# Polysketch attention and a tanh-shrink FFN on one core: the first 256 tokens head by head, a new order of the work, and 1.45 MB of loads in flight

## The chip, the core and the metric

One core of a Trainium2 chip. The metric is the device time of one execution in microseconds. Five engines take part: PE (TensorE, matmuls), DVE (VectorE), ACT (ScalarE), POOL (GpSimd) and SP (SyncE, which issues nearly all DMAs). Each works through its own queue of instructions strictly in order, and waits on semaphores where an operand comes from another engine or from a load.

## What is computed

```python
# q, k, v: 4 batches, 4 heads, 1088 tokens, 32 features; S1, S2: 8 x 32
def phi(x):                     # 64 features: products of two sketches of 8
    a = einsum('rd,bhsd->bhsr', S1, x)
    b = einsum('rd,bhsd->bhsr', S2, x)
    return einsum('bhsi,bhsj->bhsij', a, b).reshape(..., 64)
q_p, k_p = phi(q), phi(k)
kv  = einsum('bhsf,bhsd->bhfd', k_p, v)
z   = sum(k_p, axis=2)
num = einsum('bhsf,bhfd->bhsd', q_p, kv)
den = einsum('bhsf,bhf->bhs', q_p, z) + 1e-6
x   = (num / den), heads side by side       # 4352 tokens x 128
h   = x @ w_in                              # 128 x 2048
out = (h - tanh(h)) @ w_out                 # 2048 x 128, float32
```

Every key of a batch enters its kv, so that no token of a batch can be finished before all its keys and values are there.

## The kernel before

All matmuls of the attention are float32 in small tiles of the array (32x32, 64x32, 128x32); those of the FFN are bf16 on the whole array. The kernel first records all operations with their operands, and then a table (`TABLE`) lists them one by one in a global order; each token names the operation, the engine that gets it (v DVE, a ACT, g POOL, t PE, s SP) and, after the colon, the buffers. `f` and `F` are filler matmuls on zeros. From the table every engine gets its queue, and the waits follow from the operands and the buffers.

Loads stand in SP's queue in the table's order. `plan` also makes a load wait until the loads issued before it have landed but for the newest ones, so that no more than `CAP` bytes are in flight:

```python
if o.big:
    left = CAP - o.dma[0]
    for p in reversed(loads):
        left -= p.dma[0]
        if left < 0:
            o.deps.setdefault(p, False)
            break
    loads.append(o)
```

For each batch (b = 0 to 3) the attention runs through these steps; the names are those that the text uses, with batch and place (kT2, qp1.5), and the lines are those of the profile:

- keys: load kL (L438), turn on DVE (kT, L528), sketch on PE (ksk, L548), turn on DVE (abk, two instructions, L554; called kab in the order);
- gram matrix on PE (gram, L569), copy (gm, L579), the denominators' weights on PE (scmm, L575), copy into the query weights (L581);
- products of the two key sketches (w, three pieces of 128x768, L589, on DVE or POOL), kv on PE (kvmm, three pieces, L604, into one bank, 128x64);
- kv into the form that the numerator needs: copied four times side by side (kvd), transposed by PE (kvt, L622), copied (kvb);
- queries: load qL, turn on DVE (qT, L540), sketch on PE (qsk, L643), turn on DVE (abc, L648); products and sums for the denominator (m L660, den L663), reciprocal (rd, L666), scaled half (ap, L668; called aq in the order); products (qp, L686), turned (qpT, L691);
- numerator on PE (num, L702, which writes four banks), and two copies into xT in bf16 (L349).

Numerators come in pieces of whole blocks of 128 tokens: batch 0 has (0, 2), (2, 5) and (5, 9); batch 1 (0, 5) and (5, 9); batches 2 and 3 one. Batch 0's first 256 tokens have a query load, sketch and products of their own.

The weights: wi and wo are loaded as float32 in four pieces each and cast to bf16; wi is transposed by PE (wit, L767; copies wiT), and `w_in @ w_out` is made from both (wc, L781) and split into two bf16 parts (wch, wcl L788), because `h - tanh(h)` times w_out is computed as `x @ (w_in @ w_out)` plus `tanh(-h) @ w_out`. wc lies in one of the three banks that the hidden layer uses, until wcl has read it.

The FFN runs over ten groups of tokens (256, 384, 448, six of 512, 192), numbered 0 to 9. A group has 16 hidden matmuls (h, L802), 16 tanh on ACT (th, L806; from group 7 on two at a time), and 18 output matmuls (o, L817 and L821) that collect in one bank, which DVE turns (ot, L826) and SP stores in four DMAs (st, L836). Group 0 needs the tokens 0 to 256, group 1 those to 640, group 2 those to 1088 (all of batch 0), group 3 those to 1600. In the table of before, the kv work of batches 1, 2 and 3 (kT, ksk, abk, w, kvmm, kvt) stands between group 0's end and group 2's beginning.

Of the kernel before, what the change touches and what calls it, by code (L numbers as in the profile page):

```python
# [4 lines left out]
B, H, S, D = 4, 4, 1088, 32  # L5
# [18 lines left out]
TABLE = """
0v 50g 14s 13a 10g 1g 15s 6g 2g 16s 17s 18s 19s 20s 59v:0 21s 4v 22s 60v 23s 61v 48v 5v 51g 62v 8g 52g 7g 49v f F F F
F F F F F F F 64t:0 58g 24s 3g 25s 65v:0 63v 66v F F F F F F 67t:0 71v:0 68a:0 f F 69t 72v:1 74t:1 70a 80t:0 75t 73v:2
26s 225a 81v:0 F F 233t:0 27s 226a 82g:0 11g 28s 83v:0 234t 227a 84v:0 29s 85g:0 76t 86g:0 236t:1 30s 77a:0 31s 78t
229a 53g 12g 87v:0 228g 79a:0 32s F F 88t:0 235a 55g 91v 237t 89a 90a 230g 33s 100t:0 238a 245t:0 231g 34s 247t:2
101v:1 246a:0 249t:1 248a:1 251t:0 232g 35s 250a:2 253t:2 277t:0 252a:3 36s 255t:1 278t 102v:0 254a:4 257t:0 37s
256a:5 259t:2 103v:1 279t 258a:6 261t:1 38s 260a:7 104v:1 263t:0 262a:8 39s 105g:1 265t:2 264a:9 239t:1 280t 266a:10  # L30
54g 267t:0 56g 106v:1 240t 40s 269t:2 268a:11 281t 282t 270a:12 271t:0 111g:2 283t 284t 107v:1 241t 272a:13 41s 285t
273t:2 286t 287t 42s 275t:0 274a:14 113g:0 108t:0 112v:0 276a:15 43s 242t 114v 109a 44s 110a 115t:0 118v:1 45s 119v
46s 300t:0 302t:2 116a 288t 47s 157v:0 120t:0 301a:16 243a 303a:17 289t 244v 92s 304t:0 290t 121v:1 291t 306t:1
305a:18 292t 122v 293t 307a:19 117v 127g:3 158v 294t 308t:0 310t:1 295v:0 159t:0 128g:4 309a:0 296s 311a:1 312t:0 93s
332t:0 160v:0 333t 94s 313a:2 334t 314t:1 136v 129g:5 316t:2 95s 318t:0 315a:3 335t 130t:0 297s 317a:4 96s 123t:2 161v
319a:5 131t 97s 124a:1 162t:1 166g:0 298s 191v:1 132t 299s 125t 336t 98s 192v 320t:0 126a 133a:1 337t 99s 322t:1 9g
168v:1 321a:6 134t 193t:1 323a:7 167g:2 163a:0 135a:1 324t:0 338t 194v:1 339t 325a:8 326t:1 328t:2 195v 169t:0 327a:9
200v:3 196t:2 329a:10 170t 164t 171t 201v:4 165a 340t 330t:0 341t 342t 202v:5 331a:11 203t:1 197a:1 204t 172v:0 198t
205t 175v 199a 173t 206a:1 343t 344t 207t 174a:2 355t:0 209v 357t:1 208a:3 345t 137t:0 356a:12 358a:13 359t:0 361t:1
138v:0 346t 360a:14 347t 363t:2 348t 362a:15 349t 365t:0 364a:16 367t:1 176t:0 350v:1 139g:0 366a:17 351s 368a:18  # L40
387t:0 140v:0 369t:0 352s 388t 389t 141v:0 353s 370a:19 371t:1 390t 142v:0 354s 373t:2 372a:0 391t 177v:1 143g:1 392t
374a:1 375t:0 393t 377t:1 376a:2 394t 395t 378a:3 379t:2 396t 145g:2 144v:1 397t 380a:4 398t 399t 381t:0 383t:1 57g
400t 150g:0 146v 382a:5 385t:2 401t 384a:6 147t:0 386a:7 152g:1 151v:0 402t 403t 149v 148a 404t 153v 410t:0 412t:1
414t:2 178v:1 411a:8 154t:0 413a:9 179v:1 415a:10 180v:1 416t:0 181g:1 155v 418t:1 156a 420t:2 417a:11 405v:2 210t:0
182g:2 419a:12 406s 422t:0 421a:13 442t:0 407s 211v:0 424t:1 423a:14 426t:2 408s 443t 425a:15 444t 409s 428t:0 445t
427a:16 184v:0 446t 430t:1 429a:17 447t 432t:2 212g:0 183v:1 431a:18 448t 434t:0 433a:19 449t 436t:1 213v:0 450t
435a:0 438t:2 214v:0 451t 437a:1 452t 186v:1 440t:0 439a:2 453t 465t:1 441a:3 454t 185v 455t 467t:2 466a:4 456t 457t
187v 468a:5 469t:0 458t 459t 470a:6 471t:1 215v:0 473t:2 460v:0 218g:2 475t:0 472a:7 188t:0 474a:8 461s 476a:9 462s
220g:0 463s 477t:0 497t:0 479t:1 464s 478a:10 498t 499t 480a:11 481t:0 216v:1 483t:2 500t 482a:12 485t:1 501t 484a:13
217v:0 502t 487t:0 486a:14 503t 489t:2 189v 504t 488a:15 505t 491t:1 490a:16 190v 493t:0 506t 492a:17 507t 219v 508t  # L50
495t:2 494a:18 520t:1 509t 496a:19 221v 510t 522t:0 521a:0 524t:2 511t 523a:1 512t 526t:1 513t 525a:2 514t 528t:0
527a:3 530t:2 515v:1 222t:0 529a:4 516s 531a:5 517s 532t:0 518s 552t:0 534t:1 533a:6 519s 536t:2 553t 535a:7 554t 555t
537a:8 538t:0 540t:1 556t 539a:9 542t:2 557t 541a:10 544t:0 558t 543a:11 559t 546t:1 560t 545a:12 548t:2 561t 547a:13
550t:0 562t 549a:14 563t 564t 579t:1 551a:15 565t 581t:2 580a:16 566t 583t:0 582a:17 585t:1 567t 584a:18 568t 569t
# [855 lines left out]
```

## Time and profile before

| | |
|---|---|
| time, three runs | 111.40, 112.95 and 112.78 us; median 112.78 |
| profiled execution | 111.28 us, span of the trace 109.1 us |
| PE busy | 97.9 us (90%) |
| ACT busy | 80.8 us (74%) |
| DVE busy | 58.4 us (54%) |
| POOL busy | 30.3 us (28%) |
| moved by DMA | 11.38 MB, mean 104 GB/s |

In the profile's rows the columns are the start in us, the duration, the engine, the line and the operation, what is written from what, the shapes, and how many instructions the row merges; in brackets stands the idle time of the engine ahead of it and what ended that. SPq is SP's queue issuing a DMA. A float32 matmul of the small tiles is shown as two. Matmuls overlap: a row of one 512-column matmul lasts 0.38 us, but the next starts 0.22 us after it. A busy PE is therefore not one at its peak.

### The profile page before, as it was taken

To read this page: it belongs to the slowest core of one execution; us is meant where nothing else is said; L and a number is where in the kernel's file an instruction comes from. 1 tells how busy PE (TensorE), PEld (TensorE's weight loads), DVE (VectorE), ACT (ScalarE), POOL (GpSimd) and SP (SyncE) were. 2 spreads that over 40 slices of the span, in tenths; PEclk is the share of its full clock that TensorE was granted. 3 is DMA by queue.
4 is the path that set the end of the run, shared out by engine and by line. 5 is a ranking of instruction groups with operands and counts; after the bars stand their busy time and mean duration, and the time that the engine had idled before them with its cause. 6 is when DMAs were issued, how large, how long until landed. Compare 5 with 4: busy or idle time off the path is not lost.

```text
span 109.1 us, 3403 instructions
## 1 busy us (share of the span) xinstructions
PE 97.9 (90%) x1460; PEld 47.9 (44%) x1467; DVE 58.4 (54%) x91; ACT 80.8 (74%) x166; POOL 30.3 (28%) x48
## 2 busy tenths in 40 slices
PE   5969867989589899999999999999999999999980
PEld 2225543564246366354434444344434444444550
DVE  0369446784874999796979999520015002020130
ACT  4001768964555646888599989996999999999970
POOL 3030453870199500249385076000000000000000
PEclk9999999999999999999999999999999999999999
DMA  3878699898869800040013014006000503201444
GB/s 84 219 232 280 220 254 300 266 248 302 261 153 320 215 13 3 6 72 0 6 25 56 9 26 71 6 0 96 0 0 12 90 1 53 43 0 28 71 62 70
DMA packets 25918, 11.38 MB, mean 104 GB/s; under 512 B 19120, under 2 KB 23600, under 8 KB 25904
## 3 DMA queue, kind: packets, MB, share of 16 engines
q1 hardware_dynamic: 25344, 11.11, 40.1%
q8 instruction: 11, 0.18, 0.7%
q10 hardware_dynamic: 560, 0.07, 0.4%
q14 instruction: 3, 0.02, 0.1%
HBM read 8.95 MB, written 2.23 MB: 102 GB/s over the span
## 4 chain that ended last, share of the span: by engine, by line
PE 54%; DMA 20%; DVE 10%; SPq 7%; POOL 3%; issue 2%
PE psb L817 22%; PE psb L802 20%; DMA wo_f<-in_moe_w_out_dram 8%; DMA kL<-in_k_dram 8%; SPq L438 7%; PE psb L702 5%; DMA wi_f<-in_moe_w_in_dram 5%; DVE kT L528 3%; PE psb L821 2%; POOL qp L686 2%; PE psb L604 2%; DVE w L589 2%; PE psb L643 1%; DVE abk L554 1%; DVE abc L648 1%
## 5 line engine op out<-in xcount | busy, mean ns | idle before, releaser
L806 ACT ACTIVATE th<-psb 128x512 bf16<-128x512 f32 (+4 forms) x136 | 70.1, 618 | 8.3 <-PE psb L802 5.8
L802 PE MATMUL psb<-xT,wi 128*128 128x512 bf16 (+4 forms) x154 | 46.3, 347 | 1.8 <-DVE wcl L788 1.0
L817 PE MATMUL psb<-th,wo 128*128 128x512 bf16 (+4 forms) x160 | 45.4, 348 | 0.4 <-issue 0.3
L802 PEld LDWEIGHTS psb<-xT,wi 128*128 128x128 bf16 x160 | 14.9, 97 | 23.8 <-ACT th L806 11.4
L826 DVE STREAM_TRANSPOSE ot<-psb 128x512 f32<-128x512 f32 (+4 forms) x10 | 6.3, 626 | 31.4 <-PE psb L817 31.4
L817 PEld LDWEIGHTS psb<-th,wo 128*128 128x128 bf16 x160 | 15.2, 98 | 13.2 <-issue 0.8
L686 POOL TENSOR_TENSOR qp<-ap,abc 128x512 f32<-128x512 f32 (+1 forms) x10 | 13.8, 1393 | 5.7 <-DVE ap L668 5.5
L691 DVE STREAM_TRANSPOSE qpT<-qp 128x768 f32<-128x768 f32 (+1 forms) x14 | 11.8, 854 | 2.8 <-POOL qp L686 2.6
L702 PE MATMUL psb<-qpT,kvb 32*32 32x128 f32 (+4 forms) x448 | 8.3, 309 | 1.7 <-ACT kvb L349 1.0
L528 DVE STREAM_TRANSPOSE kT<-kL 128x576 f32<-128x576 f32 (+3 forms) x10 | 5.9, 612 | 6.5 <-DMA kL<-in_k_dram 6.5
L589 POOL TENSOR_TENSOR w<-abk 128x768 f32<-128x768 f32 x5 | 7.5, 1518 | 5.6 <-DVE abk L554 5.6
L413 PE MATMUL psb<-zz 128*128 128x512 bf16 x21 | 7.5, 501 | 0.0
L702 PEld LDWEIGHTS psb<-qpT,kvb 32*32 32x32 f32 x448 | 5.2, 103 | 4.9 <-ACT kvb L349 1.5
L589 DVE TENSOR_TENSOR w<-abk 128x768 f32<-128x768 f32 x7 | 7.2, 1071 | 0.1
L648 DVE STREAM_TRANSPOSE abc<-psb 128x1152 f32<-128x1152 f32 (+2 forms) x5 | 5.7, 1140 | 1.8 <-PE psb L643 1.8
L660 POOL TENSOR_TENSOR m<-abc 128x288 f32<-128x288 f32 (+1 forms) x3 | 2.5, 844 | 14.4 <-DVE abc L648 14.4
L604 PE MATMUL psb<-w,vL 128*32 128x64 f32 x288 | 6.1, 222 | 0.3 <-POOL w L589 0.3
L540 DVE STREAM_TRANSPOSE qT<-qL 128x1088 f32<-128x1088 f32 (+2 forms) x5 | 5.2, 1057 | 0.9 <-DMA qL<-in_q_dram 0.9
L579 ACT COPY gm<-psb 128x32 f32<-128x32 f32 x4 | 0.8, 188 | 6.5 <-PE psb L569 6.5
L604 PEld LDWEIGHTS psb<-w,vL 128*32 128x32 f32 x288 | 4.6, 109 | 1.8 <-issue 0.6
L686 DVE TENSOR_TENSOR qp<-ap,abc 128x768 f32<-128x768 f32 x4 | 4.6, 1157 | 0.7 <-POOL ap L668 0.7
L548 PE MATMUL psb<-kT,wab 64*32 64x288 f32 x64 | 3.3, 472 | 1.7 <-DVE kT L528 0.9
(58 smaller groups left out, 63.0 us busy)
## 6 DMA issues: line engine op xcount, KB each, us to landing
vL<-in_v_dram SPq DMA_DIRECT2D x16, 144.0 KB, 3.6
kL<-in_k_dram SPq DMA_DIRECT2D x8, 272.0 KB, 4.1
qL<-in_q_dram SPq DMA_DIRECT2D x6, 272.0 KB, 4.0
wi_f<-in_moe_w_in_dram SPq DMA_DIRECT2D x4, 256.0 KB, 5.4
wo_f<-in_moe_w_out_dram SPq DMA_DIRECT2D x4, 256.0 KB, 4.2
out_dram<-ot SPq DMA_DIRECT2D x16, 64.0 KB, 2.0
out_dram<-ot SPq DMA_DIRECT2D x8, 56.0 KB, 2.6
qL<-in_q_dram SPq DMA_DIRECT2D x2, 208.0 KB, 3.8
```

The source lines that it names most:

```text
L413: "F": lambda e, n: e.matmul(bank(3), zz.ap[:, 0:128], zz.ap[:, None, 128:384].to_broadcast([128, 2, 256]), start=True, stop=True)}, zop)
L438: op = P.add({x: 180.0 + 2.1 * rows for x in (eng if isinstance(eng, tuple) else (eng,))}, lambda e, n: e.dma_start(out=o_, in_=i_), w=w, ...
L528: P.add(_v(nb * 32 * (r1 - r0)), lambda e, n, e_=e_, nb=nb, r0=r0, r1=r1: e.transpose(kT[b].ap.rearrange("p (j u t r) -> p r j u t", u=2, ...
L589: P.add({**_v(768), **_gt(768)}, lambda e, n: e.tensor_tensor(out=wv.ap.rearrange("p (x i j) -> p x i j", i=8, j=8), in0=abh(0)[:, :, :, N ...
L604: i = e.matmul(pv[b].ap[h * 32:(h + 1) * 32, 0:64], vL[b][:, h, blk * 32:(blk + 1) * 32], wvs[b, p].ap[:, (bi * 4 + h) * 64:(bi * 4 + h + ...
L648: P.add(_vp(sn * 4), lambda e, n: e.transpose(abc.ap.rearrange("p k h f -> p h k f")[:, :, 0:s1 - s0, :], psa4[:, :, 0:sn].rearrange("p h ...
L686: P.add({**_v(cn * 256), **_gt(cn * 256)}, lambda e, n, qp=qp, c0=c0, cn=cn: e.tensor_tensor(out=qp.ap[:, 0:cn * 256].rearrange("p (x i j) ...
L691: P.add(_v(cn * 256), lambda e, n, qp=qp, o0=o0, cn=cn: e.transpose(qt.ap[:, o0 * 256:(o0 + cn) * 256], qp.ap[:, 0:cn * 256]), r=[qp], w=[ ...
L702: i = e.matmul(psa4[h * 32:(h + 1) * 32, g, 0:nb * 32], kvb.ap[g * 32:(g + 1) * 32, x, h * 32:(h + 1) * 32], qq[g * 32:(g + 1) * 32, 0:nb, ...
L802: P.add(_mm(n_), lambda e, n, jb=jb, hv=hv: e.matmul(hv.ap[:, jb % m * 512:jb % m * 512 + n_], wi[jb // 4].ap[:, (jb % 4) * 128:(jb % 4 + ...
L806: P.add(_a(n_ * m), lambda e, n, hv=hv, th=th: e.activation(out=th.ap.rearrange("p (u x) -> p u x", u=m)[:, :, 0:n_], in_=hv.ap.rearrange( ...
L817: fn = lambda e, n, x=x, st=st, sp_=sp_: e.matmul(ov.ap[:, 0:n_], wo[x // 4].ap[:, x % 4, :], ths[x][0].ap[:, ths[x][1] * 512:ths[x][1] * ...
```

## The change

Batch 0's first 256 tokens get a path of their own, in which each head stays on its own 32 partitions:

- kv is turned by one DVE instruction (`kvh`) instead of kvd, kvt and kvb. These three stay, for the rest of batch 0, but later.
- The query sketch has 4 matmuls of 256 columns (before: 16 of 64), the numerator 8 of 256 columns (32 of 64), in one bank each.
- m and qp of these tokens are done by DVE (POOL before), m's input is turned by one instruction.

```python
CAP = 1.45e6                                                    # 1.3e6
PIECES = {0: [(2, 5), (5, 9)], 1: [(0, 5), (5, 9)], 2: [(0, 9)], 3: [(0, 9)]}   # batch 0 had (0, 2) too
...
kvh = _Val(ap=sb("kvh", [128, 64]))

def kv_heads():
    P.add(_vp(64), lambda e, n: e.transpose(kvh.ap, pv[0].ap[:, 0:64]), r=[pv[0]], w=[kvh], name="kvh")

def q_heads(i):
    ...
    def sk(e, n):
        for h in range(H):
            r = e.matmul(pq.ap[h * 32:(h + 1) * 32, 0:nx * 32], wqs[0][h * 32:(h + 1) * 32, :],
                         qt_.ap[h * 32:(h + 1) * 32, :], start=True, stop=True)
        return r
    ...
    def num(e, n):
        qq = qt.ap[:, 0:nx * 64].rearrange("p (c x t) -> p c x t", x=2, t=32)
        for x in range(2):
            for h in range(4):
                r = e.matmul(pn.ap[h * 32:(h + 1) * 32, 0:nx * 32], kvh.ap[h * 32:(h + 1) * 32, x * 32:(x + 1) * 32],
                             qq[h * 32:(h + 1) * 32, :, x, :], start=(x == 0), stop=(x == 1), skip_group_check=True)
        return r
...
 def attention():
     k_transposes(0)
-    q_transpose(0, 0)
     k_sketch(0)
     gram(0)
     for p in range(3):
         k_outer(0, p)
     kv_mm(0)
-    kv_tail(0)
-    st = q_front(0, 0, 2)
-    q_piece(0, 0, 0, 2, *st)
-    q_transpose(0, 1)
+    kv_heads()
+    q_heads(0)
     load_k(B - 1)
     load_q(B - 1, 0)
     load_v(B - 1)
+    q_transpose(0, 1)
+    kv_tail(0)
     st = q_front(0, 2, 9)
-    for b0, b1 in PIECES[0][1:]:
+    for b0, b1 in PIECES[0]:
         q_piece(0, 2, b0, b1, *st)
```

`TABLE` is new from end to end; the costs that `load` gets for a DMA's issue (`occ`) are other numbers, which nothing in the plan reads. What the new order holds, engine by engine:

- SP: the second half of batch 0's keys goes ahead of S2. With the larger `CAP`, the first load of wo waits for batch 0's last values instead of for the first load of wi. The store of group 0 stands in the middle of batch 2's loads (ahead of the second half of its queries and its values); batch 3's keys and queries stand among the stores of group 1, its values among those of groups 2 and 3.
- PE: `wit0, kvmm0.0 to 0.2, wit1, wit2, wit3, num0.0` (before: `kvmm0.0, qsk0.0, kvmm0.1, wit0, wit1, kvmm0.2, wit2, kvt0, num0.0`); after num0.0 three fillers and two hidden matmuls, then the second query sketch. Batch 1's key sketch comes before the numerators of batch 0's rest, batch 1's kvmm and kvt in group 1. Batch 2's gram and scmm come in group 2, its kvmm in group 3 and its kvt in group 4; batch 3's key sketch and gram come in group 3, its kvmm in group 5, its kvt between the hidden matmuls of groups 5 and 6, its numerator in group 6 (before: in group 5).
- ACT: casts all four pieces of wi (POOL did the last), does kvd0 and both copies wiT ahead of the first x copies, and casts wo's first piece after them, ahead of the first tanh.
- DVE: both masks first; batch 1's kT right after the reciprocal of batch 0's rest; wcl and the copy of group 1's x ahead of batch 2's kT; batch 3's kT between the transposes of batch 1's products (qpT1.3 and qpT1.5). It does w0.1, w0.2, w1.1, w2.0, w2.2 and the products qp0.0, qp2.6, qp3.3.
- POOL: w0.0, w1.0, w1.2, w2.1, w3.0 to 3.2 and the other products, qp0.2 among them.

150 lines of the change are left out of this document (96 added, 54 removed).

## The prediction

> **What bounds the kernel now.** I read the granted clock first (full speed in every stretch), then the busy time by stretches that I cut at marks of the work, then the timeline of each engine from the first load on, and last the groups by line and shape. The stretches run from the first hidden-layer matmul (17.62) over the first one of group 3 (53.36) to the last output tile (106.4). The columns are the stretch, its length, the busy us (and instructions) of PE, of PE's weight loads, DVE, ACT and POOL, the granted clock, and the DMA engines' share and GB/s.
>
> ```profile
> 17.62:25.78 8.16, 7.36 (x181) 4.50 (x172) 6.79 (x10) 5.50 (x18) 4.74 (x7) 1.00 0.88 279
> 25.78:34.67 8.89, 7.22 (x174) 3.79 (x171) 5.04 (x11) 5.05 (x14) 5.20 (x4) 1.00 0.83 244
> 34.67:43.24 8.57, 7.81 (x219) 4.67 (x217) 8.53 (x11) 5.00 (x17) 2.27 (x3) 1.00 0.38 108
> ...
> 72.83:106.40 33.57, 32.84 (x225) 15.51 (x228) 4.81 (x8) 31.80 (x53) 0.00 (x0) 1.00 0.24 37
> ```
>
> Late in the kernel PE is busy for 32.84 of 33.57 us, ACT for 31.80: there the end moves only if PE has less left to do there, or comes there sooner. Between 17.62 and 43.24 PE idles 3.2 us (25.62 less 7.36, 7.22 and 7.81) while ACT idles ten. That is what there is to win, with the 17.6 us ahead of it. The start, engine by engine:
>
> ```profile
> 10.83 1.97 ACT L349 CAST wi<-wi_f 128x512 bf16<-128x512 f32 x3 [0.84 <-DMA wi_f<-in_moe_w_in_dram]
> 12.16 0.40 PE L767 MATMUL psb<-identb,wi 128*128 128x128 bf16 x4 [0.22 <-ACT wi L349]
> 13.09 0.37 ACT L349 COPY kvd<-psb 128x256 f32<-128x256 f32 x1 [0.30 <-PE psb L604]
> 14.26 0.71 DVE L691 STREAM_TRANSPOSE qpT<-qp 128x512 f32<-128x512 f32 x1 [1.56 <-POOL qp L686]
> 15.22 1.01 ACT L349 COPY wiT<-psb 128x1024 bf16<-128x1024 bf16 x1
> 15.38 0.85 PE L702 MATMUL psb<-qpT,kvb 32*32 32x64 f32 x64 [0.99 <-ACT kvb L349]
> 16.27 0.43 ACT L349 CAST xT<-psb 128x128 bf16<-128x128 f32 x2
> 17.02 0.67 PE L643 MATMUL psb<-qT,wq 32*32 32x224 f32 x32 [0.46 <-DVE qT L540]
> 17.62 0.50 PE L802 MATMUL psb<-xT,wi 128*128 128x256 bf16 x3
> 17.94 3.15 ACT L806 ACTIVATE th<-psb 128x256 bf16<-128x256 f32 x11 [0.32 <-PE psb L802]
> ```
>
> The first numerator matmul (15.38) waits 0.99 us for kvb, the last of three steps (kvd, transposes, kvb). The products qpT were ready at 14.97. Then the queries' second sketch (17.02) holds the first FFN matmul back to 17.62. The middle:
>
> ```profile
> 27.68 0.78 DVE L528 STREAM_TRANSPOSE kT<-kL 128x576 f32<-128x576 f32 x1 [1.79 <-DMA kL<-in_k_dram]
> 28.70 0.34 PE L802 MATMUL psb<-xT,wi 128*128 128x384 bf16 x1 [0.96 <-DVE wcl L788]
> 31.01 3.64 DMA kL<-in_k_dram
> 43.24 0.77 PE L643 MATMUL psb<-qT,wq 32*32 32x288 f32 x32
> 44.19 1.38 DVE L648 STREAM_TRANSPOSE abc<-psb 128x1152 f32<-128x1152 f32 x1 [0.21 <-PE psb L643]
> 51.30 1.18 PE L702 MATMUL psb<-qpT,kvb 32*32 32x160 f32 x64 [0.22 <-DVE qpT L691]
> 53.36 0.59 PE L802 MATMUL psb<-xT,wi 128*128 128x512 bf16 x2 [0.22 <-issue]
> ```
>
> DVE stands 1.79 us before kT2 for its load, wcl is queued behind it, and PE then loses 0.96 waiting for wcl. The last batch's keys land at 34.65. All of the kv work of batches 1 to 3 comes before batch 1's query sketch (43.24), so that DVE and POOL begin batch 1's queries late, and group 3 opens at 53.36.
>
> **The change, part by part: the start.** The second half of the keys goes ahead of S2 on SP and the masks move ahead of the transposes on DVE: the key sketch comes some 0.6 us sooner. That is worth nothing, because PE's new order has the first weight transpose (wit0) ahead of the kv matmuls, and it needs the first cast of wi: 10.83 + 0.66 (1.97 for three) = 11.5. From there: wit0 0.4 (as at 12.16), 72 kv matmuls at 0.44 for 24 (a row of 48 stands further down) 1.3, so 13.2. DVE then turns kv itself (kvh, 128x64). Not shown on PSUM; the nearest rows are a 128x64 transpose of SBUF and the 128x256 one:
>
> ```profile
> 5.75 0.20 DVE L497 STREAM_TRANSPOSE stt<-sin 128x64 f32<-128x64 f32 x1
> 11.36 0.44 DVE L648 STREAM_TRANSPOSE abc<-psb 128x256 f32<-128x256 f32 x1
> 20.37 0.57 POOL L668 TENSOR_TENSOR ap<-abc,rd 128x224 f32<-128x224 f32 x1 [0.39 <-DVE rd L666]
> 57.90 0.92 DVE L686 TENSOR_TENSOR qp<-ap,abc 128x768 f32<-128x768 f32 x1
> 63.78 1.60 PE L702 MATMUL psb<-qpT,kvb 32*32 32x288 f32 x64
> ```
>
> Between 0.20 and 0.44; I take 0.20 for its size: 13.45. Queued behind kvh on DVE are qp (now on DVE, 512 elements at the rate of 0.92 for 768: 0.61) and qpT (0.71), with 0.1 between them: 14.9. The numerator of 8 matmuls of 256 columns has no row: not under the 0.85 of 64 short ones, not over 1.60; I take 0.95, since two of 256 columns follow each other on a tile: 15.95. ACT meanwhile casts all four wi (to 13.45), then does kvd 0.37 and both wiT, 1.01 each, ahead of the x copies: 15.9. The two meet. x copies 0.43, and the first FFN matmul is at 16.5, 1.1 sooner. Its tanh stands behind the cast of wo (0.66, as for wi): 17.1, 0.85 sooner. Bounds: 0.9 more for kvh and numerator at their upper ends, and for the load (1.45 MB in flight lets the first wo share with the first wi, 262 KB at some 250 GB/s) up to 1.05 more; the low ends of the three are what I took.
>
> **The middle.** The second sketch runs at 16.75, after two FFN matmuls. From its end to the end of ap the old timeline takes 17.69 to 20.94, 3.25 us: now 17.42 to 20.7. The 768-element product is then POOL's instead of DVE's (0.92 above):
>
> ```profile
> L686 POOL TENSOR_TENSOR qp<-ap,abc 128x768 f32<-128x768 f32 x4 | 6.7, 1692 | 5.6 <-DVE ap L668 5.5
> 28.56 0.83 DVE L554 STREAM_TRANSPOSE abk<-psb 128x288 f32<-128x288 f32 x2
> 32.09 1.25 ACT L806 ACTIVATE th<-psb 128x384 bf16<-128x384 f32 x3 [0.16 <-PE psb L802]
> ```
>
> 1.6 on POOL, 0.9 for qpT, 0.83 for batch 1's two abk transposes, which now stand ahead of the numerator: it starts at 24.0, later than before, so that the start's gain is nearly used up here. I allow 2.5 for it, its copies, gram, scmm and theirs: first tanh of group 1 at 26.4. But now PE does not stop for wcl (no kT stands before it), nor for batch 3's keys. ACT paces group 1: 15 tanh at 0.42 (1.25 for three) 6.3, four copies of some 0.37 1.5, and 0.8 of idle under PE's num and kvmm blocks: batch 1's query sketch at 34.9 instead of 43.24. From sketch to numerator the same instructions run on the same engines as before, 8.06 us (43.24 to 51.30): 43.0. PE's own work comes there at about the same time. Group 3 opened 2.06 after that numerator with three output matmuls between; now there are six, and both x copies are ACT's (0.43 as the pair at 16.27, each about that for its size): I take 2.25, 45.2 instead of 53.36.
>
> **What is handed back.** Of the kv work, batch 2's part from kvmm on and all of batch 3's now follow group 3's opening:
>
> ```profile
> 33.34 0.37 PE L569 MATMUL psb<-abk 128*32 128x32 f32 x18
> 34.34 0.23 PE L575 MATMUL psb<-gm,s2r 128*32 128x8 f32 x8
> 35.16 0.43 PE L622 MATMUL psb<-ident,kvd 128*128 128x128 f32 x2
> 36.10 0.83 PE L548 MATMUL psb<-kT,wab 64*32 64x288 f32 x16 [0.51 <-DVE kT L528]
> 40.36 0.88 PE L604 MATMUL psb<-w,vL 128*32 128x64 f32 x48
> 65.54 0.38 PE L817 MATMUL psb<-th,wo 128*128 128x512 bf16 x1 [0.16 <-issue]
> ```
>
> Two kvmm 2 x 3 x 0.44 = 2.64, gram 0.37, scmm 0.23, sketch 0.83, two kvt 0.86: 4.93. By the two orders PE also changes its tile shape 40 times after the first FFN matmul, not 30; six of the ten more lie here. A change costs PE 0.16 after a numerator (65.54) and nothing in other rows, so 0 to 0.96; I take 0.6. The Trainium skill (TensorEngine Tiling (Array Packing), Key Properties) says that changing the tiling mode drains TensorE; were each of the ten changes to cost the 0.16 as after a numerator, the sum would be about 1 us worse. The trace agrees for the numerator alone.
>
> The sum: group 3 is 8.16 us earlier, 5.53 is handed back, 2.6 is left: span 109.1 to 106.5, profiled time 111.28 to 108.7. The timed runs of before lie 0.1 to 1.7 above its profiled execution, with the median 1.5 above; I add 0.7 and forecast 109.4. The larger cap, st0 standing before batch 2's values on SP, and the other pieces of DVE and POOL work I put at nothing: the DMA engines are busy for 0.38 of the stretch from 34.67 and less later, so that this costs only where a load lands later than its reader's turn.
>
> **Rivals.** *Late joins eat it.* On DVE batch 3's kT now stands ahead of qpT for batch 1's second piece, and its load is issued only behind st1 on SP, which waits for ot1, which stands behind abc:
>
> ```profile
> 30.61 0.36 SPq L836 DMA_DIRECT2D out_dram<-ot  x1
> 45.50 0.54 DVE L826 STREAM_TRANSPOSE ot<-psb 128x384 f32<-128x384 f32 x1
> ```
>
> From the end of abc: ot1 0.54, the store's issue 0.4 (30.61 to 31.01), the first load's about as much, the second load 3.64 with its issue: 5.0. The transpose that precedes kT ends 5.7 after abc (51.30 less 45.57). The slack is 0.7, and each us beyond it comes out whole. With this load 1.5 late and the start's upper bounds (up to 1.95, of which the later waits hide half) the gain falls to 0.5 to 1.5: 110.5 to 111.5, and 113 with nothing hidden and the timed runs 1.7 above. For it: every join of the new order is tight. Against: DMA is nearly empty there.
>
> *POOL becomes the bound, slower.* POOL gets seven w (five before) and six of the 768 products (four):
>
> ```profile
> 45.66 0.80 POOL L660 TENSOR_TENSOR m<-abc 128x288 f32<-128x288 f32 x1 [8.72 <-DVE abc L648]
> 58.06 1.41 POOL L660 TENSOR_TENSOR m<-abc 128x288 f32<-128x288 f32 x1 [0.81 <-DVE abc L648]
> ```
>
> The same product takes 0.80 alone and 1.41 when it starts beside a DVE product (57.90, above) that ends at 58.82: 0.61 more. Ten POOL products stand on the chains to the numerators of batches 0 to 2; were all blocked so, 6.1 us would go, 3.5 more than is won: 114.8 profiled, 115.5. It decides from the fifth blocked product on. Against: beside most of them DVE's new order has transposes. The Trainium skill (SBUF — State Buffer, Who interferes with whom) says that VectorE instructions with two SBUF inputs and GpSimd's exclude each other for a whole instruction; the 58.06 row agrees, and by that rule only pairs of products count.
>
> *It does not do what it says.* The start is set by the first wi load and both wiT copies, whatever turns kv; if the load lands 1.05 later there is no gain in the start. This is the lower part of the first rival.
>
> **How the numbers follow.** Forecast 0.60 (gain 1.8, with the shape changes at their upper end and half a us of the start's, to 4.0, without the 0.6 and the 0.8 of idle; own range 107.3 to 111.2), late joins with the start 0.22, POOL 0.18. Two per cent, about what a measurement of this kernel tells from no change, is 2.26 us. Of the forecast 0.52 is beyond it and 0.08 within; the joins are all within; POOL is 0.02 within and 0.16 slower. The range 107.3 to 113.0 holds the first two cases and leaves out about 0.18.
>
> **What would show it.** Right: first FFN matmul near 16.5, no wait of PE for wcl, batch 1's query sketch near 35, group 3 opening near 45, then PE without gaps to about 103.5. Wrong: wi landing after 11.5, POOL rows of w and qp far above 1.7, DVE waiting for kL at batch 3's kT, PE idle before the numerators of batches 1 and 2, or PE's busy time after group 3's opening up by more than 6 us.

## The result, and the profile after

The changed kernel takes 106.46 us (median of four runs, 106.28 to 107.19) against 112.40 for the kernel before beside it (four runs, 111.40 to 112.95): 0.949 of the time, interval 0.941 to 0.958. Two further sets of six runs gave medians of 106.66 and 106.88, ratios 0.964 (0.957 to 0.971) and 0.958 (0.954 to 0.962). Faster, as forecast; but the forecast was 109.4 and its range began at 107.3. The profiled execution took 106.51 us, its span 104.7.

The first lines are again stretches (length, then busy us of PE, of its weight loads, DVE, ACT, POOL; granted clock; DMA share, GB/s), cut at the first hidden matmul, group 1's first one, batch 1's query sketch, batch 1's first numerator (42.38) and the last output tile:

```profile
15.99:25.23 9.24, 8.69 (x183) 5.04 (x182) 6.70 (x13) 6.59 (x20) 7.19 (x9) 1.00 0.85 283
25.23:34.17 8.94, 8.93 (x199) 4.83 (x193) 6.94 (x10) 7.60 (x22) 4.07 (x6) 1.00 0.51 116
34.17:42.38 8.21, 8.21 (x123) 3.63 (x122) 6.18 (x9) 7.34 (x18) 4.32 (x8) 1.00 0.48 109
42.38:101.22 58.84, 57.81 (x715) 28.63 (x722) 23.79 (x36) 53.15 (x98) 13.91 (x13) 1.00 0.26 48
```

The same last stretch of the kernel before, from batch 1's first numerator (51.30) on:

```profile
51.30:106.02 54.72, 53.79 (x522) 24.93 (x529) 21.96 (x31) 51.17 (x92) 8.68 (x7) 1.00 0.21 32
```

And its stretch from the first hidden matmul to batch 1's first numerator:

```profile
17.62:51.30 33.68, 30.23 (x665) 16.50 (x656) 27.26 (x39) 22.57 (x63) 16.35 (x18) 1.00 0.57 166
```

This part took 33.68 us before and takes 26.39 now. PE's busy time in it fell from 30.23 to 25.83 us (8.69, 8.93 and 8.21), because work was moved behind it, and its idle time from 3.45 to 0.56. Behind batch 1's numerator the changed kernel needs 58.84 us where the old one needed 54.72: 4.12 us are handed back. So what is won behind the start is nearly all idle time of PE, 2.89 us. The page's chain of work that ended last has lost its loads, and the waits of DVE for keys are down from 6.5 us to 1.9 (the first line is the chain of before, the other two are of the changed kernel):

```profile
PE 54%; DMA 20%; DVE 10%; SPq 7%; POOL 3%; issue 2%
PE 69%; DVE 18%; POOL 8%; issue 2%; DVEq 0%
L529 DVE STREAM_TRANSPOSE kT<-kL 128x576 f32<-128x576 f32 (+3 forms) x10 | 5.8, 598 | 1.9 <-DMA kL<-in_k_dram 1.9
```

The start, from the timelines of POOL, DVE, ACT and PE:

```profile
8.18 1.51 POOL L590 TENSOR_TENSOR w<-abk 128x768 f32<-128x768 f32 x1 [2.58 <-DVE abk L555]
8.35 2.16 DVE L590 TENSOR_TENSOR w<-abk 128x768 f32<-128x768 f32 x1
9.58 1.26 ACT L350 CAST wi<-wi_f 128x512 bf16<-128x512 f32 x2 [0.22 <-DMA wi_f<-in_moe_w_in_dram]
10.32 0.39 PE L825 MATMUL psb<-identb,wi 128*128 128x128 bf16 x4
10.92 1.38 PE L605 MATMUL psb<-w,vL 128*32 128x64 f32 x72 [0.21 <-DVE abc L649]
12.37 0.25 DVE L633 STREAM_TRANSPOSE kvh<-psb 128x64 f32<-128x64 f32 x1
13.47 0.71 DVE L670 STREAM_TRANSPOSE qpT<-qp 128x512 f32<-128x512 f32 x1
14.24 1.06 PE L678 MATMUL psb<-qpT,kvh 32*32 32x256 f32 x16 [0.31 <-DVE qpT L670]
15.99 0.39 PE L860 MATMUL psb<-xT,wi 128*128 128x256 bf16 x2
```

kvh took 0.25 and the numerator of 256-column matmuls 1.06, near the values that I took (0.20 and 0.95). wi's first cast began at 9.58, earlier than in the old trace (10.83), so that the first weight transpose stands at 10.32, 1.2 us earlier than I wrote (11.5). The kv matmuls then wait 0.21 us for DVE, whose product at 8.35 took 2.16 us; at the first hidden matmul 0.5 us of the 1.2 is left.

The marks of all profiles in one table (us): first wi cast, first hidden matmul, batch 1's first numerator, last output tile; "early" is the second to the third, "late" the third to the fourth. The profiles of after_again, old_order_heads and before_wcl_first come from executions over 1.5% above the fastest of their sets, so that their early parts are not compared with the others.

| kernel | wi | hidden | num1.0 | last tile | early | late |
|---|---|---|---|---|---|---|
| before | 10.83 | 17.62 | 51.30 | 106.02 | 33.68 | 54.72 |
| after | 9.58 | 15.99 | 42.38 | 101.22 | 26.39 | 58.84 |
| after_again | 9.99 | 16.03 | 43.41 | 102.24 | 27.38 | 58.83 |
| after_third | 9.94 | 15.68 | 42.58 | 101.41 | 26.90 | 58.83 |
| after_cap13 | 10.26 | 15.91 | 43.02 | 101.85 | 27.11 | 58.83 |
| new_order_old_path | 9.99 | 16.72 | 43.09 | 101.93 | 26.37 | 58.84 |
| old_order_heads | 11.00 | 17.57 | 52.24 | 106.96 | 34.67 | 54.72 |
| new_start_old_rest | 10.25 | 15.90 | 49.55 | 104.27 | 33.65 | 54.72 |
| before_wcl_first | 11.80 | 18.92 | 52.39 | 107.11 | 33.47 | 54.72 |
| before_h_twice | 10.37 | 17.59 | 51.13 | 107.80 | 33.54 | 56.67 |
| after_h_twice | 10.26 | 15.93 | 42.76 | 103.50 | 26.83 | 60.74 |
| late_kv_twice | 9.54 | 15.81 | 42.36 | 104.95 | 26.55 | 62.59 |
| late_kv_spread | 9.90 | 15.56 | 42.04 | 102.83 | 26.48 | 60.79 |
| sketch_first | 10.10 | 16.46 | 42.49 | 101.32 | 26.03 | 58.83 |
| start_w_dve | 9.17 | 15.07 | 41.57 | 100.41 | 26.50 | 58.84 |
| both_starts | 9.54 | 15.92 | 41.95 | 100.84 | 26.03 | 58.89 |

It is the most useful reading of this case. In these profiles the late part goes with the order alone and repeats to 0.06 us; what varies between executions lies ahead of batch 1's numerator. So the cost of what was moved can be read to a tenth of a us from one profile, while the times of whole runs scatter by one to more than three us.

### The profile page after: what moved, and what is told of

It is laid out like the page before. It is cut to its first block, busy times and chain, and to the rows that moved or that the text cites. A ratio compares the mean times of both kernels' runs of the same rounds, so it can differ in the third digit from the quotient of the medians.

```text
span 104.7 us, 3264 instructions
## 1 busy us (share of the span) xinstructions
PE 97.7 (93%) x1390; PEld 47.9 (46%) x1398; DVE 54.3 (52%) x89; ACT 81.5 (78%) x168; POOL 33.5 (32%) x49
## 4 chain that ended last, share of the span: by engine, by line
PE 69%; DVE 18%; POOL 8%; issue 2%; DVEq 0%
PE psb L875 24%; PE psb L860 22%; PE psb L414 5%; PE psb L761 5%; POOL qp L745 4%; DVE w L590 4%; DVE qpT L750 4%; PE psb L879 3%; DVE abc L707 2%; PE psb L605 2%; PE psb L702 2%; POOL w L590 2%; PE psb L549 2%; DVE abk L555 2%; POOL ap L727 1%
## 5 line engine op out<-in xcount | busy, mean ns | idle before, releaser
L745 POOL TENSOR_TENSOR qp<-ap,abc 128x768 f32<-128x768 f32 (+1 forms) x11 | 14.2, 1312 | 6.4 <-DVE ap L727 6.3
L590 POOL TENSOR_TENSOR w<-abk 128x768 f32<-128x768 f32 x7 | 12.0, 1713 | 7.8 <-DVE abk L555 7.8
L750 DVE STREAM_TRANSPOSE qpT<-qp 128x768 f32<-128x768 f32 (+1 forms) x13 | 10.7, 850 | 4.8 <-POOL qp L745 4.8
L414 PE MATMUL psb<-zz 128*128 128x512 bf16 x23 | 8.5, 501 | 1.1 <-DVE zz L412 1.1
L707 DVE STREAM_TRANSPOSE abc<-psb 128x1152 f32<-128x1152 f32 (+1 forms) x4 | 5.2, 1306 | 4.7 <-PE psb L702 4.7
L761 PE MATMUL psb<-qpT,kvb 32*32 32x128 f32 (+3 forms) x384 | 7.5, 323 | 0.1
L590 DVE TENSOR_TENSOR w<-abk 128x768 f32<-128x768 f32 x5 | 5.9, 1178 | 0.0
L350 ACT CAST xT<-psb 128x192 bf16<-128x192 f32 (+4 forms) x9 | 3.2, 369 | 1.9 <-PE psb L761 1.6
L414 PEld LDWEIGHTS psb<-zz 128*128 128x128 bf16 x23 | 2.5, 119 | 4.4 <-issue 2.9
L555 DVE STREAM_TRANSPOSE abk<-psb 128x288 f32<-128x288 f32 x8 | 3.4, 450 | 2.2 <-PE psb L549 2.2
```

The lines of the kernel that those rows point to most:

```text
L414: "F": lambda e, n: e.matmul(bank(3), zz.ap[:, 0:128], zz.ap[:, None, 128:384].to_broadcast([128, 2, 256]), start=True, stop=True)}, zop)
L590: P.add({**_v(768), **_gt(768)}, lambda e, n: e.tensor_tensor(out=wv.ap.rearrange("p (x i j) -> p x i j", i=8, j=8), in0=abh(0)[:, :, :, N ...
L707: P.add(_vp(sn * 4), lambda e, n: e.transpose(abc.ap.rearrange("p k h f -> p h k f")[:, :, 0:s1 - s0, :], psa4[:, :, 0:sn].rearrange("p h ...
L745: P.add({**_v(cn * 256), **_gt(cn * 256)}, lambda e, n, qp=qp, c0=c0, cn=cn: e.tensor_tensor(out=qp.ap[:, 0:cn * 256].rearrange("p (x i j) ...
L750: P.add(_v(cn * 256), lambda e, n, qp=qp, o0=o0, cn=cn: e.transpose(qt.ap[:, o0 * 256:(o0 + cn) * 256], qp.ap[:, 0:cn * 256]), r=[qp], w=[ ...
L761: i = e.matmul(psa4[h * 32:(h + 1) * 32, g, 0:nb * 32], kvb.ap[g * 32:(g + 1) * 32, x, h * 32:(h + 1) * 32], qq[g * 32:(g + 1) * 32, 0:nb, ...
```

## The experiments

### The changed kernel again, and the cap alone

after_again and after_third are the changed kernel. after_cap13 differs in one number:

```diff
-CAP = 1.45e6
+CAP = 1.3e6
```

> The changed kernel once more, beside the others of this call. Both theories of the start expect 106.5 (105.9 to 107.2). What is asked is whether the first wi cast comes at 9.6 again (before: 10.83), and whether the profiled execution lies at the median of the timed ones, as it did (106.51 against 106.46), and not 1.1 to 1.5 below it, as for the kernel before. If the offset is a matter of luck in one profile, it will differ here by half a us or more.

> The changed kernel with 1.3 MB in flight instead of 1.45. Theory: the larger cap is worth nothing, 106.5 within 0.5, the first wi cast again within 0.4 us of 9.6, because wi is issued at 5.56 either way. Rival: the cap is what let wi land 1.2 us sooner than I assumed; then the first cast is back at 10.8, the first weight transpose at 11.5, num0.0 at 15.2 instead of 14.24, and the time is 107.2 to 107.6, because PE has next to no gap behind the first hidden matmul.

after_again 106.66 (105.94 to 107.64), after_cap13 106.88 (106.24 to 107.22; ratio 0.967, 0.962 to 0.972): no difference that can be seen. The first cast of wi came at 10.26, further off than the 0.4 us that I allowed; but it came at 10.26 with the larger cap too (after_h_twice), so that the cap is not shown to move it. Here the first weight transpose waited for that cast:

```profile
10.93 0.40 PE L825 MATMUL psb<-identb,wi 128*128 128x128 bf16 x4 [1.00 <-ACT wi L350]
```

The numerator stood at 14.16 and the first hidden matmul at 15.91 all the same, since in the profile of after, where wi came 0.7 us sooner, the start waited for DVE's products instead. The two paths have nearly the same length. On the offset the chance answer was the better one: the profiles of the changed kernel lie 0.2 below to 1.0 above the medians of their sets. The larger of these is in after_again, where PE stood 1.11 us in front of batch 1's key sketch:

```profile
22.75 0.83 PE L549 MATMUL psb<-kT,wab 64*32 64x288 f32 x16 [1.11 <-DVE kT L529]
```

The keys of batch 1 came late there; behind the first hidden matmul PE waits so long for nothing in the two other profiles of this kernel.

### The head path alone, and the order without it

new_order_old_path has the new table, but the first 256 tokens go through kvd, kvt and kvb; old_order_heads has the old table with the head path set into it.

```diff
 # new_order_old_path
-kv_heads()
-q_heads(0)
+q_transpose(0, 0)
+kv_tail(0)
+st = q_front(0, 0, 2)
+q_piece(0, 0, 0, 2, *st)
 # old_order_heads: TABLE of before, in it
 #   kvmm0.2 kvh(DVE) kvd0 wiT0 qp0.0(DVE) ... num0.0 ... kvt0, kvb0 behind h0.6, th0.6
```

> The new order, cap and engines, but the first 256 tokens go the old way: kvd, kvt and kvb ahead of the numerator, the sketch of 16 short matmuls, the numerator of 64. Theory: the new order makes the gain; num0.0 stands at 14.2 to 14.6, set by qp and qpT as before, because kvd, kvt and kvb (0.37, 0.43 and 0.37, from 12.35 on) end by then; the first hidden matmul is 0 to 0.6 later: 106.5 to 107.2. Rival: the head path carries the 1.63 us that the start won, num0.0 is at 15.4 as before: 107.8 to 108.3.

> The old order with 1.3 MB in flight, and in it only the head path for the first 256 tokens (kvh, the short sketch and numerator, m and qp on DVE; kvd at its old place, kvt and kvb after the seventh hidden matmul). Theory: the order is what counts; num0.0 comes 0.3 to 1.0 sooner, batch 1's query sketch still stands behind all kv work near 42.5 to 43.2, group 3 opens near 53, and the time is 111.4 to 112.6. Rival: the head path is the gain, 107.5 to 110.8.

new_order_old_path 107.20 (106.74 to 108.99; ratio 0.969, 0.963 to 0.975); old_order_heads 111.99 (110.32 to 113.23; ratio 1.005, 0.999 to 1.011), no change. In the old order the head path brought the numerator to 14.94 instead of 15.38, and the gain ended in front of the second query sketch, which waited for its queries and stood ahead of the first hidden matmul:

```profile
14.94 1.07 PE L678 MATMUL psb<-qpT,kvh 32*32 32x256 f32 x16 [0.93 <-DVE qpT L670]
...
16.96 0.67 PE L702 MATMUL psb<-qT,wq 32*32 32x224 f32 x32 [0.63 <-DVE qT L541]
17.57 0.39 PE L860 MATMUL psb<-xT,wi 128*128 128x256 bf16 x2
```

In the new order the old path let the numerator begin at 13.99, as early as the head path does (13.93 to 14.24). It then stopped in its middle:

```profile
13.99 0.53 PE L761 MATMUL psb<-qpT,kvb 32*32 32x64 f32 x34
15.67 0.40 PE L761 MATMUL psb<-qpT,kvb 32*32 32x64 f32 x30 [1.14 <-issue]
```

For 1.14 us PE waited for nothing that the profile shows, and the first hidden matmul came at 16.72. What the stop is stays open. So kvh is not what makes the numerator early; the head path is worth at most the half us between the medians of 107.2 and 106.7, and the intervals of the two overlap. The order is the change.

### The start alone

new_start_old_rest takes the new table up to the third tanh of group 0, and from there the remaining operations in the order and on the engines of before.

```diff
 # TABLE: tokens of after up to th0.2,
 #        then those of before that are not yet listed
```

> The changed kernel's order up to the third tanh of group 0 (head path, loads, casts, the start on all engines), and from there the order of the kernel before, with its engines. Theory: the gain is made by the order behind the start; the first hidden matmul stands at 15.9 to 16.1 as after the change, but the kv work of batches 2 and 3 stands again ahead of group 3, which opens at 51.7 (if the start's 1.6 is passed on whole) to 53.4 (if the waits for keys eat it): 109.9 to 111.6, that is 0.97 to 1.0 of before. Rival: the start makes most of it, 107 to 109.

109.61 (109.02 to 110.65; ratio 0.979, 0.972 to 0.986), a little below the 109.9 that I had as the best case. The start's 1.72 us (15.90 against 17.62) were passed on whole: the early part took 33.65 us, as before. The loads that I thought would eat it moved up with it. So of the 8.92 us by which batch 1's numerator came sooner in the first profile, 1.6 come from the start and 7.3 from the order behind it, which then gives 4.12 back: by these marks of single profiles the two halves of the change gain 1.6 and 3.2.

### What the moved work costs

late_kv_twice issues on PE twice what was moved behind group 3's opening: kvmm2, kvmm3, gram3, scmm3, ksk3, kvt2, kvt3.

```diff
-for h in range(4):
-    i = e.matmul(pv[b].ap[..., 0:64], vL..., wvs...)
+for h in range(4):
+    if b >= 2:
+        e.matmul(pv[b].ap[..., 256:320], vL..., wvs...)
+    i = e.matmul(pv[b].ap[..., 0:64], vL..., wvs...)
 # likewise gram, scmm and ksk for b == 3, kvt for b >= 2
```

> The changed kernel with the kv work that the change put behind group 3's opening issued twice on PE: both kvmm of batches 2 and 3 (36 more matmuls each), gram, scmm and the key sketch of batch 3, both kvt. The results are the same; the copies write columns that nobody reads or the same values. It measures the term of my sum that I called handed back. By my sum of rows it costs 4.93 us (111.5). Theory of the miss: rows carry the filling and emptying of the array, and whole blocks last 3.99 (1.21 x 2 for kvmm, 0.37 for gram and scmm, 0.76, 0.22 x 2), so 3.6 to 4.1 more (110.1 to 110.8). Rival: gaps of PE in the late part hide some of it, under 3 us (109.6 or less).

110.16 (109.89 to 110.64; ratio 0.984, 0.979 to 0.989). The late part grew from 58.84 to 62.59, by 3.75 us, inside the 3.6 to 4.1 of the theory and well off the 4.93 of my sum. The rows show why. The key sketch of 16 is a row of 0.83 us; 32 of them last 1.48, so that the second 16 cost 0.65. Two kvt are a row of 0.43 in the old trace; four last 0.60, and the next matmul begins 0.44 after the first:

```profile
47.10 1.48 PE L549 MATMUL psb<-kT,wab 64*32 64x288 f32 x32
48.51 0.61 PE L870 MATMUL psb<-xT,wi 128*128 128x512 bf16 x2
...
56.53 0.60 PE L633 MATMUL psb<-ident,kvd 128*128 128x128 f32 x4
56.97 0.38 PE L870 MATMUL psb<-xT,wi 128*128 128x512 bf16 x1
```

A row's duration runs to the end of its last matmul, and the next work begins before that.

### What a change of the tile shape costs

late_kv_spread has the same instructions as the changed kernel, with hidden and output matmuls between the pieces.

```diff
-h3.12 h3.13 h3.14 kvmm2.0 gram3 kvmm2.1 kvmm2.2 scmm3 h3.15 o3.9
+h3.12 kvmm2.0 h3.13 gram3 h3.14 kvmm2.1 h3.15 kvmm2.2 o3.9 scmm3
-o4.16 o4.17 h5.9 kvmm3.0 kvmm3.1 kvmm3.2 h5.10
+o4.16 kvmm3.0 o4.17 h5.9 kvmm3.1 h5.10 kvmm3.2
```

> The changed kernel with the same instructions, but the pieces of kvmm, gram and scmm behind group 3's opening are taken apart: between them stand hidden and output matmuls, so that PE changes its tile shape twelve times more. From batch 1's first numerator to the last output tile the changed kernel takes 58.84 us. If a change costs the 0.1 that I took (0.6 for six), this takes 60.0; if it costs the 0.16 seen behind numerators each time, 60.8; if the next matmuls overlap with the end of the last shape's, 58.7 to 59.1, and the time stays at 106.5.

108.37 (107.80 to 108.87; ratio 0.972, 0.968 to 0.976) beside after_third's 106.88; the late part 60.79, 1.95 us more, the highest of the three cases by its size. Not all of it is the changes: scmm3 waited for gm, which I had put behind kvd2 on ACT, for some 0.4 us. The rest, about 1.55, is 0.13 for each of twelve. Batch 3's part, where no such wait lies, says the same:

```profile
68.05 0.38 PE L875 MATMUL psb<-th,wo 128*128 128x512 bf16 x1
68.36 0.54 PE L605 MATMUL psb<-w,vL 128*32 128x64 f32 x24
69.06 0.38 PE L860 MATMUL psb<-xT,wi 128*128 128x512 bf16 x1 [0.16 <-issue]
69.37 0.54 PE L605 MATMUL psb<-w,vL 128*32 128x64 f32 x24
69.84 0.39 PE L860 MATMUL psb<-xT,wi 128*128 128x512 bf16 x1
70.16 0.54 PE L605 MATMUL psb<-w,vL 128*32 128x64 f32 x24
70.86 0.59 PE L875 MATMUL psb<-th,wo 128*128 128x512 bf16 x2 [0.16 <-ACT th L864]
```

From 68.05 to 70.86 are 2.81 us, in which by the order o4.16, o4.17, h5.9, h5.10 and h5.11 start too, five of 0.2155 us, the distance at which such matmuls follow each other (four from 83.06 to 83.92 in the old trace; only three of the five have a row): 1.73 for the three pieces apart. Together in the changed kernel they took 1.24:

```profile
67.36 0.38 PE L860 MATMUL psb<-xT,wi 128*128 128x512 bf16 x1
67.66 1.21 PE L605 MATMUL psb<-w,vL 128*32 128x64 f32 x72
69.03 0.38 PE L860 MATMUL psb<-xT,wi 128*128 128x512 bf16 x1 [0.16 <-issue]
69.25 0.59 PE L875 MATMUL psb<-th,wo 128*128 128x512 bf16 x2
```

(69.03 less 67.36, less two of h5.9, h5.10 and h5.11, of which one has no row.) 0.5 more for four changes is 0.12 each. That it is the shape and not the change from bf16 to float32 and back, the kvt in late_kv_twice show: they are float32 between bf16 matmuls on the whole array, two cost 0.22 us (54.54 to 54.76 in the changed kernel) and four 0.44, with nothing fixed on top. The Trainium skill (TensorEngine Tiling (Array Packing), Key Properties) says that a change of the tiling mode drains TensorE; this run agrees and gives it a price here, 0.12 to 0.13 us.

The last fence holds a trap into which I went. The 0.16 "issue" behind kvmm3 looks like a drain. By the order, h5.10 and h5.11 stand between kvmm3.2 and o5.0, and only one of them has a row. Their weight loads have both:

```profile
68.80 0.11 PEld L860 LDWEIGHTS psb<-xT,wi 128*128 128x128 bf16 x2
```

The page of the changed kernel lists 160 of these weight loads and 152 of the matmuls. In the old trace it is the same behind batch 2's numerator: the row at 65.54, from which the prediction took its 0.16, is o4.0, and h4.6, which stands ahead of it, is missing (its weight load is there, at 65.31). Where the record was not lost, in new_start_old_rest, the next matmul is a hidden one 1.54 us after the numerator's start, with no gap:

```profile
62.03 1.60 PE L761 MATMUL psb<-qpT,kvb 32*32 32x288 f32 x64
63.57 0.39 PE L860 MATMUL psb<-xT,wi 128*128 128x512 bf16 x1
```

### Is PE the bound late in both kernels?

Nine hidden matmuls of groups 4 to 6 issued twice, in the changed kernel and in the one before:

```diff
-lambda e, n, ...: e.matmul(hv..., wi..., xt, start=True, stop=True)
+lambda e, n, ...: [e.matmul(hv..., wi..., xt, start=True, stop=True)
+    for _ in range(2 if gi in (4, 5, 6) and jb % 5 == 2 else 1)][-1]
```

> The changed kernel with nine hidden matmuls of groups 4, 5 and 6 issued twice, 512 columns each, one every 0.2155 us: 1.94 us more of PE. Theory: behind group 3's opening PE sets the time, 1.7 to 2.0 more (108.4 to 108.7). Rival: ACT, busy for 51.7 of 56.4 us there, sets it in parts, 0.5 to 1.3 more.

> The kernel before with the same nine matmuls twice. Theory of the miss: the kernel before has 0.7 us of PE idle behind group 3's opening, where ACT is busy for 50.3 of 52.7 us, and takes up some of any work put there: 0.9 to 1.5 more than before. Rival: PE sets its end just as much, 1.7 to 2.0 more; then the idle there is no part of why less was handed back.

after_h_twice 108.47 (108.00 to 108.80); its late part 60.74, 1.90 more. before_h_twice 113.45 (113.03 to 115.32; ratio 1.012, 1.007 to 1.018) beside 112.12; its late part 56.67 against 54.72, 1.95 more for 1.94 of work. The medians alone would have pleased my theory of slack in the old kernel's end (1.33 more); the late parts refute it. PE is the bound there in both.

### Is the wait for wcl worth anything by itself?

```diff
 # DVE
-kT2.0.0 wcl ... kT2.1.0
+wcl kT2.0.0 ... kT2.1.0
```

> The kernel before, with wcl ahead of both parts of batch 2's kT on DVE, nothing else changed. Of the order's gain ahead of batch 1's numerator I counted the wait of PE for wcl (0.96 us) as won, because no kT stands before it any more. If that wait has a worth of its own, 0.7 to 1.0 us less than before, and batch 1's numerator at 50.3 to 50.6 instead of 51.30. Rival: PE only comes sooner to the next wait (batch 2's kT at 30.30, batch 3's keys at 36.10), so that nothing is left of it: 51.1 to 51.4 and no change. I hold the rival the likelier: the keys of batch 3 land when they land.

111.80 (110.12 to 112.55; ratio 0.995, 0.990 to 1.000). The wait is gone, and the next one has grown:

```profile
29.49 0.27 PE L821 MATMUL psb<-xT,wcl 128*128 128x256 bf16 x1
...
31.40 0.83 PE L548 MATMUL psb<-kT,wab 64*32 64x288 f32 x16 [0.94 <-DVE kT L528]
```

In the old trace PE stood 0.35 us there:

```profile
30.30 0.84 PE L548 MATMUL psb<-kT,wab 64*32 64x288 f32 x16 [0.35 <-DVE kT L528]
```

0.59 of the 0.96 us have only moved to the next wait. This is read in one of the three profiles whose early parts are not to be compared, so that the split holds for this execution alone; the times decide. The rival has the better of it, though the interval of the times does not exclude a gain of up to 1%.

### Three faster starts

sketch_first moves one operation, start_w_dve gives two to other engines, both_starts does both:

```diff
 # sketch_first: PE
-num0.0 F F F h0.0 h0.1 qsk0.2
+num0.0(bank 3) qsk0.2 h0.0 h0.1
 # start_w_dve
-w0.0 on POOL, wo0 on ACT
+w0.0 on DVE, wo0 on POOL
```

> The changed kernel with the second query sketch right behind the first numerator, ahead of the first two hidden matmuls, in the place of the three fillers, and the first numerator in bank 3 so that the sketch's banks are free. If PE is the bound from the first hidden matmul on, the sketch's 0.66 us move into a gap: batch 1's numerator comes 0.4 to 0.7 sooner after the start and the time is 105.8 to 106.2. Rival: the sketch waits for the load of its queries (their transpose began between 14.26 and 15.84 in the runs of the same order), and holds up the hidden matmuls when it is late: 106.4 to 107.2.

> The changed kernel with batch 0's first product w on DVE instead of POOL (where it ran beside DVE's second one, which took 2.16 us instead of 0.91), and the cast of wo's first piece on POOL instead of ACT. Theory: three products on DVE one behind the other take 2.7 us, from 8.3 to 11.5 with a transpose between, so that kv and everything up to the first hidden matmul come 0.2 to 0.4 sooner: 106.0 to 106.4. Rival: the first wi load sets the first weight transpose at 10.3 to 10.9, and kvmm stands behind it: nothing won, 106.4 to 106.8.

> The changed kernel with both edits of the start at once: batch 0's first w on DVE and the cast of wo's first piece on POOL; the second query sketch ahead of the first hidden matmul, in the place of the three fillers. Alone they gave 106.32 and 106.19. If their gains add up: batch 1's first numerator near 41.3 and 105.6 to 106.0. If the load of the queries (their transpose began at 14.4 and 14.8) sets the sketch and so the first hidden matmul, one of them is lost: 106.1 to 106.4.

> The changed kernel a third time, for its times on the same chip as the two others. Expected: 106.5 (106.2 to 106.9); batch 1's first numerator between 42.3 and 43.5, as in the two profiles so far, and 58.84 us from there to the last output tile.

sketch_first 106.19 (105.97 to 107.00; ratio 0.953, 0.949 to 0.957), at the upper end of what its theory gave. Its early part of 26.03 is no gain: the sketch now lies ahead of the first hidden matmul, which came at 16.46, behind a wait of the sketch for its queries of 0.41 us, as the rival said, and batch 1's numerator stood at 42.49, among the 42.38 to 43.41 of the changed kernel. start_w_dve 106.32 (105.69 to 106.97; ratio 0.953, 0.948 to 0.957); its numerator came at 13.32 and the first hidden matmul at 15.07, further ahead than I expected:

```profile
7.71 1.79 DVE L590 TENSOR_TENSOR w<-abk 128x768 f32<-128x768 f32 x2
```

Two products in 1.79 us on DVE alone, where DVE's one beside POOL's took 2.16. POOL's ran from 8.18 to 9.69 in the changed kernel, and DVE's then needed 0.82 us more, about the 0.91 of one alone. The blocked product is the lock of which my second rival spoke, and in the start it lies on the path. The Trainium skill (SBUF — State Buffer, Who interferes with whom) gives the pair of ports to one of the two engines for a whole instruction; the rows agree. But only a part of the 0.9 us by which the numerator came sooner is the lock's: DVE's products also began 0.64 us sooner in that profile (7.71 instead of 8.35), and wi was there sooner (9.17). The better pair is both_starts, where the products and wi's first cast (9.54) begin as in the profile of after:

```profile
8.34 1.79 DVE L590 TENSOR_TENSOR w<-abk 128x768 f32<-128x768 f32 x2
...
13.94 1.07 PE L678 MATMUL psb<-qpT,kvh 32*32 32x256 f32 x16
```

There the numerator comes 0.30 us sooner than at 14.24. both_starts 106.29 (105.81 to 108.77; ratio 0.951, 0.947 to 0.956): the gains did not add up; the sketch waited for its queries, whose transpose began at 14.21, and held the hidden matmuls at 15.92. Beside it after_third took 106.88 (106.23 to 107.20; ratio 0.958, 0.954 to 0.962). The medians of the three are 0.1 to 0.7 us below those of the changed kernel's three sets (106.46, 106.66 and 106.88), and their ratios of 0.951 to 0.953 lie among its own (0.949, 0.964 and 0.958): none is shown to beat it.

## Why the prediction was right in sign and wrong in size

**What bounds the kernel.** Right. PE idles 0.56 us between the first hidden matmul and batch 1's numerator, and the nine doubled matmuls show it as the bound behind.

**The start.** First hidden matmul at 15.99 instead of 16.5. The error is at the head of the chain: the first weight transpose stood at 10.32, not 11.5, because I carried wi's landing over from the old trace. Most of this was lost again in that profile, since the kv matmuls did not follow the transpose but waited for DVE until 10.92, behind a product that POOL blocked; my chain had left this path out. In after_again, after_third and after_cap13 the chain was as I wrote it: the first weight transpose waited for wi's cast (10.61 to 10.93), and the kv matmuls followed. wi is issued at 5.6 in both orders; its first cast came at 9.17 to 10.26 in the new starts and at 10.37 to 11.80 in the old. The cap is not shown to be the reason, and what is stays open. The bounds that I put on kvh and on the numerator were not needed.

**The middle.** Query sketch of batch 1 at 34.17 (34.9 forecast), its numerator at 42.38 (43.0), group 3's opening at 44.85 (45.2). No wait of PE for wcl, no wait of DVE at batch 3's kT. All within 0.8 us, and within the 1.0 by which executions differ there. But the number of the query sketch came out by another way than I counted it. I let ACT pace group 1; from 25.23 to 34.17 PE is busy for 8.93 of 8.94 us and ACT for 7.60, so PE is the pace. That PE's own work would come there at about the same time I had said without a sum, so that this mark was hit in part by luck. From sketch to numerator I carried over 8.06 us of DVE's and POOL's chain, and it took 8.21: PE is busy for all of it, and the last product that the numerator needs was turned at 42.33, 0.05 us before it. My list of which waits were won was poorer than the sum: the wcl wait is worth little by itself. That PE has other work now when a load or a product is late fits the 2.89 us of idle time that are gone; which move won how much of it no run shows.

**What is handed back: the step that failed.** From batch 1's numerator on I had 5.72 us more than before (4.93 for the kv work, 0.6 for shape changes, 0.19 for the later opening). It is 4.12. The 4.93 were row durations added up. By starts, from one bf16 matmul to the next less 0.2155 for each of these, the same blocks cost 0.86 (ksk3, 46.60 to 47.89 with two of them), 1.46 (kvmm2 with gram3 and scmm3, 51.14 to 53.46 with four, of which h3.15 has no row), 1.24 (kvmm3, above) and 0.43 (two kvt):

```profile
46.60 0.59 PE L860 MATMUL psb<-xT,wi 128*128 128x512 bf16 x2 [0.16 <-issue]
47.89 0.61 PE L860 MATMUL psb<-xT,wi 128*128 128x512 bf16 x2
...
51.14 0.81 PE L860 MATMUL psb<-xT,wi 128*128 128x512 bf16 x3
53.46 0.38 PE L879 MATMUL psb<-xT,wcl 128*128 128x512 bf16 x1 [0.16 <-issue]
```

Together that is 3.99 with the shape changes in it, where I had 5.53; issued a second time the work cost 3.75. The changes' 0.6 lies between the 0.24 by which these two differ and the 0.7 to 0.8 that six cost at late_kv_spread's price, though the row that I gave for it was an artefact. So the sum of rows is what was too large, by 1.2 us (4.93 against 3.75). Three output matmuls that also moved behind the numerator are 0.57 us of work, of which 0.41 shows (group 3 opens 2.47 us behind the numerator, 2.06 before), and a stall that the old order had at the end of group 5 is gone. There o6.0 needed the bank that DVE was still reading (its weight load, at 82.18, waits for DVE's ot), and three hidden matmuls did not cover it:

```profile
81.21 0.98 PE L802 MATMUL psb<-xT,wi 128*128 128x512 bf16 x3
82.19 0.61 PE L817 MATMUL psb<-th,wo 128*128 128x512 bf16 x2
...
81.41 0.72 DVE L826 STREAM_TRANSPOSE ot<-psb 128x512 f32<-128x512 f32 x1 [8.26 <-PE psb L817]
```

Three hidden matmuls start and the next work follows 0.98 us later, 0.33 more than three need. In the changed kernel batch 3's numerator stands there and covers DVE's ot (76.61). 3.99 and 0.41 less 0.33 is 4.07, beside the 4.12 measured.

**From the span to the time.** I added 0.7 us because two of the three times shown lay 1.5 above the profile. In four later sets the kernel before had medians of 111.53, 112.12, 111.77 and 111.47, 0.2 to 0.8 above its profiled 111.28, and the medians of the changed kernel's sets lie 1.0 below to 0.2 above its profiles. The 0.7 was a reading of three numbers, and for the changed kernel it was wrong by all of it.

The miss of 2.94 us adds up: 0.62 in the early part, 1.60 handed back too much, 0.75 for the offset, and 0.03 the other way in what lies behind the last tile and around the span.

**The rivals.** Late joins: no profile of the new order shows DVE or PE waiting for batch 3's keys. The loads that came late were others: PE stood 1.11 us for batch 1's keys in after_again, and 0.46 and 0.64 us for batch 0's second queries in after_third and after_cap13. POOL as the bound: the lock is there, in products of 2.28 and 2.13 us that I had listed as a sign,

```profile
30.81 2.28 POOL L590 TENSOR_TENSOR w<-abk 128x768 f32<-128x768 f32 x1 [3.79 <-DVE abk L555]
51.88 2.13 POOL L590 TENSOR_TENSOR w<-abk 128x768 f32<-128x768 f32 x1 [1.46 <-DVE abk L555]
```

but PE did not wait for them. The place where it costs is DVE's own product in the start, by 0.3 us. "It does not do what it says" holds in one sense: the head path, after which the change is named, is worth at most half a us, and nothing in the old order.

## What to carry to other kernels

On a pipelined engine, price work that is moved by the distance of starts around its block, never by the sum of its rows' durations: here the sum was too high by a quarter to a third (4.93 us against 3.99 and 3.75). Before a gap is believed, hold the rows against the order of instructions; a lost record of one matmul looks like a stall (0.16 us here), and the count of the weight loads gives it away. And when a kernel is cut at a mark behind which all executions agree to 0.06 us, a question on size behind that mark is settled by one profile, where the times of whole runs would need many.

## What the runs showed that I had not expected

PE stopped for 1.0 to 1.1 us with nothing to wait for in two of the sixteen profiles: inside the numerator of new_order_old_path (above), and between two matmuls of kvmm in old_order_heads:

```profile
42.16 0.24 PE L605 MATMUL psb<-w,vL 128*32 128x64 f32 x1 [1.05 <-issue]
```

No run here tells what it is. That the Trainium skill (Perfetto Trace Analysis, Tensor Engine Instruction (MATMUL, LD_WEIGHTS)) calls the end time of a matmul an estimate fits what the doubled rows show: starts can be added, ends cannot.
